# The S4D convolution and gated GLU kernel: one inverse stage in the first half's product, a second queue for some spectrum stores, and stage 1 in two PSUM pools

## The chip, the cores and the metric

The kernel runs on one core of a Trainium2 chip. The metric is the device time of one execution in microseconds (us), the median of three runs. Before the change it is 693.52 us (692.16 to 694.05). One further execution was taken with the profiler; its own time is 693.17 us.

## The reference, cut to what matters

The output is a gated mix of two branches over 2048 positions (L) and 448 channels (D). With u of shape 2048 x 448:

```python
g = sigmoid((u * gate_w).sum(-1, keepdims=True))
# branch a: S4D, a convolution as long as the sequence, N = 256 states per channel
K  = 2 * einsum("dn,dnl->dl", C, exp(A * dt * l)).real          # 448 x 2048
ya = irfft(rfft(u.T, 4096) * rfft(K, 4096))[:, :2048].T + u * D_skip
# branch b: GLU, F = 1792
yb = (sigmoid(x @ w_gate) * (x @ w_up)) @ w_down
out = g * ya + (1 - g) * yb
```

All data are float32.

## The kernel before, in words

**The work.** The channels are taken in two halves, h=0 and h=1, of 224 channels. For each half the kernel generates the filter K in 14 chunks (28 in all): TensorE multiplies small tables (tile `tp`), ScalarE turns them (lines L1228 to L1246), VectorE forms products (L1253, L1267, L1270), and TensorE contracts over the states into the tile `kp` (L1282). ScalarE evicts that to `ke` (L1303), and when a half's 14 chunks are there, four DMAs store it to the DRAM tensor `kd` (one tensor for each half, `kd0` and `kd1`; each store has 2048 rows of 56 floats). These 28 chunks fill the time from about 125 to 511 us. I call what follows the last `kp` the tail.

**The convolution** is a Fourier transform in two stages, a product of spectra, and the transform back. The class `Chain` does it for one half:
- `stage1` loads `kd` into `x` (named `fx_fu` for h=0 and `fx_fk` for h=1; 8 DMAs) and the tables `ft`, and runs eight blocks `stage1_four` (TensorE L813, ScalarE eviction L816).
- `transpose` turns 32x32 pieces of `x`: for h=0 through DRAM (four stores to `shf`, four loads, L832 to L836), for h=1 on VectorE (L827).
- `product` runs eight blocks `product_four` (L877 to L894). A block makes the second stage (TensorE L846, two PSUM tiles, z=0 and 1), multiplies the spectrum of u, `ua`, by it (VectorE L880), applies the first inverse stage (TensorE L890) and evicts (ScalarE L763). The spectrum of u lies in `ua` twice: in `ua[:, 0]`, and with real and imaginary rows exchanged in `ua[:, 1]`. A complex product is therefore two real products, and L890 adds them up in PSUM by two matrices that stand side by side in `m_sb`: eight matmuls a block, each of which the trace shows as two records (x16).
- `transpose` once more, then `back` (TensorE L927, VectorE L931) adds the result to the output.

PSUM tiles of the h=0 chain are in the pool `fups`, those of the h=1 chain in `fkps`. The trace names tiles by pool: `fps_fups` is a PSUM tile of h=0, `fps_fkps` one of h=1; `uax_fk` is h=0's `ua` and `ua_fk` h=1's.

**The GLU** fills TensorE between these steps: `glu_up` (tile `gu`, L1400 to L1405, 128x512 matmuls) and `glu_down` (tile `dn`, L1419 to L1423). ScalarE takes the tanh (L1384) and the casts; the weights and x are split into a high and a low part (L1365, L1367; L1332 to L1339).

**What sets the order.** Every step is registered by `op(engine, cost, ...)`. The table `PLACE` gives each step its place in its engine's queue, by (engine, tag, priority); `Plan.order` walks the queues and emits instructions in that order, and each engine runs its own in order. All DMAs are issued by SP (`dma`, L711), one after the other.

**The start.** `ones_pro` is set by VectorE (L1026); 48 matmuls on it (L1031) keep TensorE busy until the first GLU weights and x are there. The product code of `product_four`, word for word:

```python
for z in range(2):
    op("DVE", c_dve(2 * D, False), lambda z=z: V.tensor_mul(
        ua[:, :, z], ua[:, :, z], p[z][:, :D].unsqueeze(1).to_broadcast([128, 2, D])),
       [p[z]], [(ua, (c, z)) for c in range(2)], prio)
```

Of the kernel before, what the change touches and what calls it, by code (L numbers as in the profile page):

```python
# [28 lines left out]
    ('Act', 'aci', 10): (11, 39,),  # L29
    ('Act', 'aci', 19): (61, 88,),  # L30
    ('Act', 'acr', 10): (15, 37, 46,),
    ('Act', 'acr', 19): (63, 84, 98,),
# [26 lines left out]
    ('Act', 'dots', 1): (28,),  # L59
    ('Act', 'dots', 2): (50,),  # L60
    ('Act', 'dots', 16): (80, 81,),
# [18 lines left out]
    ('Act', 'idn', 10): (17,),  # L80
    ('Act', 'junk', 10): (34, 59,),
    ('Act', 'junk', 19): (76, 78, 113,),
# [12 lines left out]
    ('Act', 'pos_sb', 10): (65, 74,),  # L95
# [250 lines left out]
MOVE = True  # L346
# [357 lines left out]
def gated_mix(ctx: ExitStack, tc, u, ut, aim, cre, cim, ldt, dskip, gw,  # L704
# [60 lines left out]
    class Chain:  # L765
# [10 lines left out]
        def psum(self, k=0):  # L776
            return self.ps[k].tile("fps", self.bufs["fps"], (128, 512))
# [783 lines left out]
```

## Time and profile before

| | us |
|---|---|
| median of three runs | 693.52 |
| the profiled execution's own time | 693.17 |
| its span, first to last instruction | 691.4 |
| around the span (693.17 - 691.4) | 1.8 |
| TensorE (PE) busy | 678.0 |
| VectorE (DVE) busy | 603.4 |
| ScalarE (ACT) busy | 513.7 |
| GpSimd (POOL) busy | 276.4 |

The mean clock that TensorE was granted is 0.994 of full speed. A busy time is the time in which an engine worked; one that is busy over nearly the whole span leaves little room for waits. The chain of waits is the list of work that ended last, followed back from the end. Names in the trace leave buffer numbers out.

### The profile page before, as it was taken

How to read it: one execution, taken by the hardware profiler on the slowest of the kernel's cores; microseconds unless marked ns; L12 is line 12 of the kernel's file. 1: busy time of each engine (PE TensorE's matmuls, PEld its weight loads, DVE VectorE, ACT ScalarE, POOL GpSimd, SP SyncE). 2: the span in 40 equal slices, each digit the busy share in tenths (PEclk: the TensorE clock that was granted, in tenths of full speed). 3: DMA queues.
4: the chain of work that ended last, by engine and by line, in shares of the span. 5: the costliest groups of instructions: out<-in, count | busy, mean ns of one | idle time of the engine just before them, and what ended most of it. 6: DMA issues, size and time to landing. Idle time of an engine off the chain costs nothing.

```text
span 691.4 us, 16303 instructions
## 1 busy us (share of the span) xinstructions
PE 678.0 (98%) x6588; PEld 485.0 (70%) x6588; DVE 603.4 (87%) x705; ACT 513.7 (74%) x934; POOL 276.4 (40%) x280
## 2 busy tenths in 40 slices
PE   8999999999999999999999999999999999999996
PEld 7766667877876687675556667778878766556874
DVE  5999999999999999999999788999973479667976
ACT  5587799899999999999999999999942351342110
POOL 0215458556467758584665745758000000000000
PEclk9999999999999999998999999999999999999999
DMA  9768442646886784859966885355947973879966
GB/s 261 190 161 220 111 125 52 169 118 246 193 172 153 183 201 127 241 169 221 170 167 182 215 230 124 103 210 156 190 104 184 247 254 139 281 251 247 183 171 172
DMA packets 98771, 126.11 MB, mean 182 GB/s; under 512 B 31240, under 2 KB 81096, under 8 KB 97672
## 3 DMA queue, kind: packets, MB, share of 16 engines
q1 hardware_dynamic: 98696, 125.07, 69.2%
q8 instruction: 52, 0.85, 0.5%
q14 instruction: 23, 0.19, 0.1%
HBM read 81.46 MB, written 43.58 MB: 181 GB/s over the span
## 4 chain that ended last, share of the span: by engine, by line
PE 83%; ACT 9%; DVE 3%; DMA 2%; issue 1%; SPq 0%; ACTq 0%; DVEq 0%
PE gu_gps L1400 11%; PE gu_gps L1401 10%; PE gu_gps L1402 10%; PE dn_gps L1419 8%; PE kp_egp L1282 6%; PE dn_gps L1421 4%; PE tp_egp L1224 4%; PE dn_gps L1422 4%; PE dn_gps L1423 4%; PE tp_egp L1233 4%; PE fps_fups L813 3%; PE gu_gps L1404 3%; PE gu_gps L1405 3%; PE fps_fups L846 2%; PE fps_fups L890 2%; PE fps_fkps L890 2%
## 5 line engine op out<-in xcount | busy, mean ns | idle before, releaser
L1400 PE MATMUL gu_gps<-xs_glu,wh_glu 128*128 128x512 f32 x336 | 146.9, 437 | 0.4 <-DVE hh_glu L1386 0.3
L1401 PE MATMUL gu_gps<-xs_glu,wh_glu 128*128 128x512 f32 x336 | 132.4, 394 | 0.0
L1402 PE MATMUL gu_gps<-xs_glu,wl_glu 128*128 128x512 f32 x336 | 132.3, 394 | 0.0
L1270 DVE TENSOR_TENSOR cs_eg<-cs_eg,es_eg 128x2048 f32<-128x2048 f32 x56 | 130.3, 2326 | 1.3
L1214 POOL TENSOR_TENSOR tb_eg<-tb_eg 128x96 f32<-128x96 f32 (+2 forms) x84 | 115.0, 1372 | 5.9
L1253 DVE TENSOR_TENSOR es_eg<-tb_eg 128x1024 f32<-128x1024 f32 x112 | 111.4, 1016 | 2.2
L1400 PEld LDWEIGHTS gu_gps<-xs_glu,wh_glu 128*128 128x128 f32 x336 | 63.5, 189 | 29.7 <-issue 12.6
L1384 ACT ACTIVATE sg_glu<-gu_gps 128x512 f32<-128x512 f32 x56 | 34.0, 607 | 63.5 <-PE gu_gps L1405 60.4
L1267 DVE TENSOR_TENSOR cs_eg<-cs_eg,es_eg 128x1024 f32<-128x1024 f32 x56 | 70.6, 1260 | 10.9 <-ACT cs_eg L1246 7.7
L1230 ACT ACTIVATE nn_eg<-cs_eg 128x512 fp32r<-128x512 f32 x112 | 72.6, 648 | 6.0 <-PE tp_egp L1233 4.6
L1401 PEld LDWEIGHTS gu_gps<-xs_glu,wh_glu 128*128 128x128 f32 x336 | 63.6, 189 | 15.9 <-issue 5.6
L1402 PEld LDWEIGHTS gu_gps<-xs_glu,wl_glu 128*128 128x128 f32 x336 | 63.4, 189 | 15.0 <-DVE wl_glu L1367 0.5
L1217 POOL TENSOR_TENSOR tb_eg<-tb_eg,bs_eg 128x32 f32<-128x32 f32 x84 | 70.4, 841 | 5.8
L1228 ACT ACTIVATE cs_eg<-tp_egp 128x512 f32<-128x512 f32 x112 | 68.6, 618 | 3.2 <-DVE og L958 2.0
L1236 ACT ACTIVATE cs_eg<-tp_egp 128x512 f32<-128x512 f32 x112 | 68.4, 616 | 1.7 <-PE tp_egp L1233 1.5
L1235 ACT ACTIVATE cs_eg<-tp_egp 128x512 f32<-128x512 f32 x112 | 68.2, 618 | 1.5 <-PE tp_egp L1233 1.1
L1438 DVE SCALAR_TENSOR_TENSOR ob_glu<-dn_gps,og,ob_glu 128x448 f32<-128x448 f32 x72 | 48.7, 677 | 23.3 <-PE dn_gps L1423 21.3
L1246 ACT ACTIVATE cs_eg<-cs_eg,half_pi 128x1024 f32<-128x1024 f32 x56 | 66.1, 1180 | 0.5
L1204 POOL MEMSET tb_eg<- 128x96 f32 x28 | 7.8, 286 | 131.6 <-DVE es_eg L1253 124.2
L1282 PEld LDWEIGHTS kp_egp<-cs_eg 128*32 128x32 f32 x3584 | 51.3, 110 | 11.0 <-issue 8.6
L1282 PE MATMUL kp_egp<-cs_eg 128*32 128x64 f32 x3584 | 55.8, 220 | 0.1
L1421 PE MATMUL dn_gps<-vh_glu,hh_glu 128*128 128x448 f32 x136 | 52.3, 384 | 0.8 <-DVE ob_glu L1438 0.8
(161 smaller groups left out, 1338.7 us busy)
## 6 DMA issues: line engine op xcount, KB each, us to landing
shf<-fx_fu SPq DMA_DIRECT2D x16, 896.0 KB
fx_fu<-shf SPq DMA_DIRECT2D x16, 896.0 KB
us<-fx_fu SPq DMA_DIRECT2D x16, 896.0 KB
xr_glu<-in_w_dram SPq DMA_DIRECT2D x52, 256.0 KB
uax_fk<-us SPq DMA_DIRECT2D x16, 448.0 KB
ua_fk<-us SPq DMA_DIRECT2D x16, 448.0 KB
xr_glu<-in_w_dram SPq DMA_DIRECT2D x17, 224.0 KB
gt_pre<-in_u_dram SPq DMA_DIRECT2D x8, 448.0 KB
```

The costliest lines, as they stand in the source:

```text
L1214: pool(96 * m, lambda n=n, m=m: G.tensor_mul(g3(n + 1, m), g3(1, m), g3(n, 1).to_broadcast([128, 32, 3, m])))
L1217: pool(32, lambda e=e: G.tensor_mul(t(e + 1), t(e), b(3)))
L1228: op("Act", c_act(512, True), lambda: S.activation(cs[:, 1, ds, 32:96], block(tp), AF.Copy, bias=MAGIC), [tp], [(cs, ("s", i))], prio)
L1230: op("Act", c_act(512), lambda: S.activation(block(nn), cs[:, 1, ds, 32:96], AF.Copy, scale=-1.0, bias=MAGIC), [(cs, ("s", i))], [nn], prio)
L1253: V.tensor_mul(o.rearrange("p d (i k) -> p d i k", k=ny), x.unsqueeze(3).to_broadcast([128, 16, nx, ny]), y.unsqueeze(2).to_broadcast([128 ...
L1267: op("DVE", c_dve(1024), lambda: V.tensor_mul(cs[:, :, :, 0:32], cs[:, ::-1, :, 63:31:-1], es[:, :, 0:32].unsqueeze(1).to_broadcast([128, ...
L1270: op("DVE", c_dve(2048), lambda: V.tensor_mul(cs[:, :, :, 32:96], cs[:, :, :, 32:96], es[:, :, 32:96].unsqueeze(1).to_broadcast([128, 2, 1 ...
L1282: T.matmul(kp[32 * j:32 * j + 32, q], cs[:, z, 4 * j + q, 64:96], cs[:, z, 4 * j + q, 0:64], start=cs is parts[0] and z == 0 and q == 0, s ...
L1400: T.matmul(p.real, wh[:, k, cs], x[:, k], start=(k == 0), stop=False)
L1401: T.matmul(p.real, wh[:, k, cs], x[:, 4 + k], start=False, stop=False)
L1402: T.matmul(p.real, wl[:, k, cs], x[:, k], start=False, stop=False)
L1421: T.matmul(p[:, :D], hh[:, ts], vh.real, start=(i == 0), stop=False)
```

## The change

1. **The product of h=0** (`SWAP = (0,)`). Instead of two accumulated matrices, the sum of the two real products is made ahead of the inverse stage. ScalarE copies the spectrum tile from PSUM to a new SBUF tile `sw`, in four activations of 32 partitions each, that exchange neighbouring groups of 32 partitions and set the sign (L918). VectorE multiplies `ua[:, 0]` by the spectrum (L921), `ua[:, 1]` by `sw` (L923), and adds (L925), each 128x448. TensorE then applies one matrix: four matmuls a block (L933) instead of eight. The product of h=1 stays as it was (its line is now L905).
2. **The stores of `kd1`** with j=1 and j=3 are issued from ScalarE's queue; j=0 and 2 stay on SP.
3. **Stage 1 of h=1**: its blocks with odd b take their PSUM tiles from `fups` instead of `fkps` (`ks[1].other`).
4. **The first GLU loads**: x and w pieces are interleaved (`glu_first`).
5. **`PLACE`** is written anew as a whole, so every queue's order differs somewhat.

Lines of the changed kernel that the text speaks of: L825 stage 1, L858 second stage, L770 eviction, L969 back, L1068 `ones_pro`, L1458 to L1463 `gu`, L1479 to L1481 `dn`.

```diff
-    ('SP', 'kd1', 20): (267, 266, 268, 265,),
+    ('Act', 'kd1', 20): (827, 823,),
+    ('SP', 'kd1', 20): (262, 263,),
...
-    def dma(dst, src, size, r, w, prio, rate=ROW, issue=400.0, **kw):
-
-        return op("SP", size / rate, lambda: nc.sync.dma_start(dst(), src()), r=r, w=w, prio=prio, size=size,
+    def dma(dst, src, size, r, w, prio, rate=ROW, issue=400.0, eng="SP", **kw):
+
+        queue = nc.scalar if eng == "Act" else nc.sync
+        return op(eng, size / rate, lambda: queue.dma_start(dst(), src()), r=r, w=w, prio=prio, size=size,
...
+        def psum_one(self, b):
+            if self.other is None or b % 2 == 0:
+                return self.psum()
+            return self.other.tile("fps", FPS, (128, 512))
...
-            x, ps = self.x, [self.psum(), self.psum()]
+            x, ps = self.x, [self.psum_one(b), self.psum_one(b)]
...
             x, prio, p = self.x, self.prio, self.spectrum_four(b)
+            if self.h in SWAP:
+                self.product_swapped(ua, b, p)
+                return
...
+        def product_swapped(self, ua, b, p):
+            prio = self.prio
+            for z in range(2):
+                sw = self.tile("sw", (128, D))
+
+                def turn(z=z, sw=sw):
+                    for a in range(4):
+                        S.activation(sw[32 * a:32 * a + 32], p[z][32 * (a ^ 1):32 * (a ^ 1) + 32, :D], AF.Copy,
+                                     scale=1.0 if a % 2 else -1.0)
+                op("Act", 4 * PIECE, turn, [p[z]], [sw], prio)
+                op("DVE", c_dve(D, False), lambda z=z: V.tensor_mul(ua[:, 0, z], ua[:, 0, z], p[z][:, :D]),
+                   [p[z]], [(ua, (0, z))], prio)
+                op("DVE", c_dve(D), lambda z=z, sw=sw: V.tensor_mul(sw.real, ua[:, 1, z], sw.real),
+                   [(ua, (1, z))], [sw], prio)
+                op("DVE", c_dve(D), lambda z=z, sw=sw: V.tensor_add(ua[:, 0, z], ua[:, 0, z], sw.real),
+                   [sw], [(ua, (0, z))], prio)
+            y = [self.psum(1), self.psum(1)]
+
+            def f():
+                for z in range(2):
+                    for i in range(2):
+                        rows, to = slice(64 * i, 64 * i + 64), slice(64 * (i ^ z), 64 * (i ^ z) + 64)
+                        T.matmul(y[z][to, :D], m_sb[rows, 64:128], ua[rows, 0, z], start=True, stop=True)
+            op("PE", c_mm64(D), f, [(ua, (0, 0)), (ua, (0, 1)), m_sb], y, prio)
...
                 dma(lambda j=j: kd[hh].v("(a b) (j e) -> j a b e", b=64, j=4)[j], lambda j=j: ke[32 * j:32 * j + 32],
-                    32 * 64 * 224, [ke], [(kd[hh], j)], prio, SHORT, 3000.0)
+                    32 * 64 * 224, [ke], [(kd[hh], j)], prio, SHORT, 3000.0,
+                    "Act" if hh == 1 and j % 2 else "SP")
...
+    def glu_first(prio):
+        x = xs[0, 0] = glu.tile("xs", 2, (128, 7, 512), F32R)
+        parts = glu_w_parts(0, 0, prio)
+        for k in (0, 2):
+            glu_xk(x, k, 0, slice(0, 256), 0, prio)
+            next(parts)
+            glu_xk(x, k, 1, slice(256, 512), 256, prio)
...
-    glu_x(0, 0, 0)
-    glu_w(0, 0, 0)
+    glu_first(0)
...
+    ks[1].other = fups
     for h in halves:
         ks[h].stage1([kd[h]], lambda h=h: kd[h].v("(a b) d -> a b d", b=32))
         ks[h].transpose()
-        if h == 0 and MOVE:
-            ks[h].move(fk, (fups, fups), SX)
+    ks[0].move(fk, (fups, fups), SX)
+    for h in halves:
         ks[h].product(us[h])
```

**What the new order moves, at three places.** In the rows below a name ends in its buffer's number, `x2` counts equal instructions in a row, and no time is in them. First TensorE, at the inverse stage of the seventh and the second stage (L846, now L858) of the eighth of h=0's product blocks. Before (the four L890 rows of each half stand as two here, each of which comes twice):

```order
L890 MATMUL fps_fups_7318<-uax_fk_7190,m_sb 64x448 x2
L890 MATMUL fps_fups_7319<-uax_fk_7190,m_sb 64x448 x2
...
L890 MATMUL fps_fkps_7334<-ua_fk_7228,m_sb 64x448 x2
L890 MATMUL fps_fkps_7335<-ua_fk_7228,m_sb 64x448 x2
...
L846 MATMUL fps_fups_7347<-fx_fu_5148,m_sb 64x448 x2
L846 MATMUL fps_fups_7348<-fx_fu_5148,m_sb 64x448 x2
L846 MATMUL fps_fkps_7358<-fx_fk_6583,m_sb 64x448 x2
L846 MATMUL fps_fkps_7359<-fx_fk_6583,m_sb 64x448 x2
```

And of the change:

```order
L905 MATMUL fps_fkps_7387<-ua_fk_7270,m_sb 64x448 x2
L905 MATMUL fps_fkps_7388<-ua_fk_7270,m_sb 64x448 x2
...
L933 MATMUL fps_fups_7405<-uax_fk_7234,m_sb 64x448 x2
L933 MATMUL fps_fups_7406<-uax_fk_7234,m_sb 64x448 x2
L858 MATMUL fps_fkps_7416<-fx_fk_6545,m_sb 64x448 x2
L858 MATMUL fps_fkps_7417<-fx_fk_6545,m_sb 64x448 x2
L858 MATMUL fps_fups_7427<-fx_fu_5149,m_sb 64x448 x2
L858 MATMUL fps_fups_7428<-fx_fu_5149,m_sb 64x448 x2
```

The inverse stage of h=0 has two rows for a block where it had four; h=1's is as it was. Between a block's second stage and its inverse stage lies the multiply, here that of the seventh block. Before, VectorE had for a block of each half only:

```order
L880 TENSOR_TENSOR uax_fk_7190<-uax_fk_7190,fps_fups_7285 128x2x448
L880 TENSOR_TENSOR uax_fk_7190<-uax_fk_7190,fps_fups_7286 128x2x448
L880 TENSOR_TENSOR ua_fk_7228<-ua_fk_7228,fps_fkps_7295 128x2x448
L880 TENSOR_TENSOR ua_fk_7228<-ua_fk_7228,fps_fkps_7294 128x2x448
L1392 TENSOR_TENSOR hl_glu_7332<-sg_glu_7025,hh_glu_7311 128x512
```

and now (`7333` and `7334` are the block's two spectrum tiles; in brackets what a row waits for: Activation is ScalarE, DMAHW a DMA):

```order
L921 TENSOR_TENSOR uax_fk_7234<-uax_fk_7234,fps_fups_7333 128x448 [waits DMAHW4_49,PE_49,Activation_49]
L895 TENSOR_TENSOR ua_fk_7270<-ua_fk_7270,fps_fkps_7344 128x2x448 [waits DMAHW6_49,DMAHW1_49,PE_49]
L921 TENSOR_TENSOR uax_fk_7234<-uax_fk_7234,fps_fups_7334 128x448
L923 TENSOR_TENSOR swx_fk_7349<-uax_fk_7234,swx_fk_7349 128x448 [waits DMAHW0_49]
L895 TENSOR_TENSOR ua_fk_7270<-ua_fk_7270,fps_fkps_7343 128x2x448
L925 TENSOR_TENSOR uax_fk_7234<-uax_fk_7234,swx_fk_7349 128x448 [waits DVE_49]
L923 TENSOR_TENSOR swx_fk_7368<-uax_fk_7234,swx_fk_7368 128x448 [waits Activation_49]
L925 TENSOR_TENSOR uax_fk_7234<-uax_fk_7234,swx_fk_7368 128x448 [waits DVE_49]
```

The first multiply of a spectrum tile waits for ScalarE: it does not read the tile while ScalarE's four copies of it run.

Second, SP around the stores of `kd1`, before:

```order
L713 DMA kd_61<-ke_eg_4122 2048x1x56 x4
L713 DMA xr_glu_6550<-in_w_dram 128x448
L713 DMA xr_glu_6554<-in_w_dram 128x512
L713 DMA xr_glu_6560<-in_w_dram 128x512
L713 DMA fx_fk_6583<-kd_61 64x4x224
L713 DMA ft_fk_6588<-in_s1t_dram 128x512
```

and now on SP:

```order
L720 DMA kd_61<-ke_eg_4120 2048x1x56 x2
L720 DMA xr_glu_6483<-in_w_dram 128x512
L720 DMA xr_glu_6489<-in_w_dram 128x512
L720 DMA fx_fk_6545<-kd_61 64x4x224
L720 DMA ft_fk_6551<-in_s1t_dram 128x512
L720 DMA ft_fk_6559<-in_s1t_dram 128x512
L720 DMA fx_fk_6545<-kd_61 64x4x224 x5
```

with the other two stores on ScalarE, where they now stand between the GLU's own steps:

```order
L1345 ACTIVATE ke_eg_4120<-kp_egp_6357 128x4x64
L720 DMA kd_61<-ke_eg_4120 2048x1x56
L1449 ACTIVATE hh_glu_6458<-sg_glu_6428 128x512
L1423 ACTIVATE vh_glu_6466<-xr_glu_6015 128x448
L1442 ACTIVATE sg_glu_6473<-gu_gps_6436 128x512
```

SP's stores are halved, and the eight loads of `kd1` follow one another instead of standing between loads of `ua` and of weights.

Third, VectorE's first rows, before:

```order
L1184 MEMSET phs 1x512
L1026 MEMSET ones_pro_97 112x128
L1336 TENSOR_TENSOR xs_glu_136<-xr_pre_92,xs_glu_136 128x2x256
L1338 TENSOR_TENSOR xs_glu_136<-xr_pre_99,xs_glu_136 128x256
L1339 TENSOR_TENSOR xs_glu_136<-xr_pre_99,xs_glu_136 64x256
L1478 MEMSET half_pi 128x1
```

and now:

```order
L1068 MEMSET ones_pro_91 112x128
L1425 TENSOR_TENSOR wl_glu_139<-xr_pre_123,wh_glu_137 128x512
L1389 TENSOR_TENSOR xs_glu_135<-xr_pre_96,xs_glu_135 128x2x256
L1389 TENSOR_TENSOR xs_glu_135<-xr_pre_125,xs_glu_135 128x2x256
L1391 TENSOR_TENSOR xs_glu_135<-xr_pre_127,xs_glu_135 128x256
L1392 TENSOR_TENSOR xs_glu_135<-xr_pre_127,xs_glu_135 64x256
```

The memset of `phs` no longer stands ahead of that of `ones_pro`, and the first weights' low part comes ahead of x's.

More of the change, by code (lines that the diff above doesn't have):

```diff
@@ L28 @@
 PLACE = {
[L29 to L32, printed above, removed]
[26 rows of a table removed]
-    ('Act', 'dots', 1): (28,),
-    ('Act', 'dots', 2): (50,),
-    ('Act', 'dots', 16): (80, 81,),
[18 rows of a table removed]
-    ('Act', 'idn', 10): (17,),
-    ('Act', 'junk', 10): (34, 59,),
-    ('Act', 'junk', 19): (76, 78, 113,),
[12 rows of a table removed]
-    ('Act', 'pos_sb', 10): (65, 74,),
[22 rows of a table removed]
-    ('DVE', 'aci', 10): (50,),
-    ('DVE', 'aci', 19): (105,),
+    ('Act', 'aci', 10): (14, 38,),
+    ('Act', 'aci', 19): (61, 85,),
+    ('Act', 'acr', 10): (15, 36, 45,),
+    ('Act', 'acr', 19): (63, 83, 100,),
[26 rows of a table added]
+    ('Act', 'dots', 1): (27,),
+    ('Act', 'dots', 2): (46,),
+    ('Act', 'dots', 16): (79, 84,),
[18 rows of a table added]
+    ('Act', 'idn', 10): (16,),
+    ('Act', 'junk', 10): (28, 58,),
+    ('Act', 'junk', 19): (75, 77, 115,),
[13 rows of a table added]
+    ('Act', 'pos_sb', 10): (60, 74,),
[6 rows of a table added]
+    ('Act', 'swx', 40): (855, 856, 861, 862, 871, 872, 880, 881, 887, 889, 895, 897, 904, 905, 913, 914,),
[16 rows of a table added]
+    ('DVE', 'aci', 10): (43,),
+    ('DVE', 'aci', 19): (115,),
     ('DVE', 'acr', 10): (82,),
-    ('DVE', 'acr', 19): (150,),
+    ('DVE', 'acr', 19): (153,),
     ('DVE', 'ai', 10): (73,),
[14 rows of a table removed]
-    ('DVE', 'dtp', 10): (40,),
-    ('DVE', 'dtv', 10): (26,),
[6 rows of a table removed]
[14 rows of a table added]
+    ('DVE', 'dtp', 10): (56,),
+    ('DVE', 'dtv', 10): (33,),
[6 rows of a table added]
     ('DVE', 'f', 10): (14, 15,),
[2 rows of a table removed]
[2 rows of a table added]
     ('DVE', 'gs', 2): (119,),
[4 rows of a table removed]
-    ('DVE', 'half_pi', 0): (4,),
[24 rows of a table removed]
-    ('DVE', 'ones', 10): (1,),
-    ('DVE', 'p', 10): (18, 20, 21, 22, 23, 24, 25,),
-    ('DVE', 'phs', 20): (0,),
[6 rows of a table removed]
-    ('DVE', 'skip', 20): (35,),
[6 rows of a table removed]
-    ('DVE', 'uax', 40): (540, 544, 551, 552, 567, 565, 576, 575, 582, 581, 588, 587, 594, 595, 600, 599, 629, 630,
[26 rows of a table removed]
[4 rows of a table added]
+    ('DVE', 'half_pi', 0): (26,),
[24 rows of a table added]
+    ('DVE', 'ones', 10): (0,),
+    ('DVE', 'p', 10): (16, 17, 23, 25, 27, 29, 31,),
+    ('DVE', 'phs', 20): (8,),
[6 rows of a table added]
+    ('DVE', 'skip', 20): (49,),
+    ('DVE', 'swx', 40): (548, 547, 560, 561, 577, 574, 587, 588, 598, 600, 608, 611, 618, 621, 632, 634,),
[6 rows of a table added]
+    ('DVE', 'uax', 40): (546, 550, 545, 549, 559, 562, 558, 563, 575, 578, 570, 579, 585, 589, 586, 590, 594, 599,
[27 rows of a table added]
         1032, 1035, 1038, 1039, 1042,),
     ('PE', 'fps', -1): (0,),
[43 rows of a table removed]
[43 rows of a table added]
     ('Pool', 'bsx1', 10): (5, 11,),
@@ L346 @@
 MOVE = True
-SX = {'ft': 1, 'ua': 2, 'fps': 2}
-SK = {'ft': 2, 'ua': 2, 'fps': 3}
+SX = {'ft': 1, 'ua': 2, 'fps': 2, 'sw': 2}
+SK = {'ft': 2, 'ua': 2, 'fps': 3, 'sw': 2}
+SWAP = (0,)
+PIECE = 540.0
 K0D, LASTG, TN, TBB = False, 1, 4, 2
@@ L475, in run @@
         if o["size"]:
-            self.free[e] = t + (o["issue"] if e == "SP" else self.CAST)
+            self.free[e] = t + o["issue"]
             self.wire = max(self.wire, self.free[e] + 1000.0) + o["cost"]
@@ L769, in __init__ @@
             self.pool, self.ps, self.bufs, self.h, self.prio, self.on_dve = pool, (ps, ps), bufs, h, prio, on_dve
-            self.suffix = ""
+            self.suffix, self.other = "", None
             self.x = pool.tile("fx", 1, (128, 32, HD))
@@ L894, in product_four @@
                 evac(lambda r=2 * b + z: self.pair(r), y[z], [(x, 2 * b + z)], prio)
+        def product_swapped(self, ua, b, p):
[20 more added lines that the diff above has]
+            op("PE", c_mm64(D), f, [(ua, (0, 0)), (ua, (0, 1)), m_sb], y, prio)
+            for z in range(2):
+                evac(lambda r=2 * b + z: self.pair(r), y[z], [(self.x, 2 * b + z)], prio)
         def back(self, q):
@@ L1317, in glu_x @@
             glu_xz(x, z, t0, prio)
+    def glu_first(prio):
[5 more added lines that the diff above has]
+            glu_xk(x, k, 1, slice(256, 512), 256, prio)
+        for _ in parts:
+            pass
     def glu_xz(x, z, t0, prio):
@@ L1344, in glu_w, with glu_w_parts @@
     def glu_w(H, f, prio):
+        for _ in glu_w_parts(H, f, prio):
+            pass
+    def glu_w_parts(H, f, prio):
         wh, wl = (glu.tile(t, WB, (128, 4, 256), F32R) for t in ("wh", "wl"))
@@ L1354, in glu_w @@
             glu_split(wr, lambda wr=wr: wr.real, wh, wl, lambda t, k=k: t[:, k:k + 2], k, 512, prio, 7 * H + f // 2)
+            yield
         ws[H, f] = (wh, wl, vh, vl)
```

517 rows, old and new, of the table PLACE are left out of this document.

## The prediction

> **What bounds the kernel now.** I read the page's busy times first, then its slices, then the busy times by stage, then the chain of waits.
>
> ```profile
> span 691.4 us, 16303 instructions
> PE 678.0 (98%) x6588; PEld 485.0 (70%) x6588; DVE 603.4 (87%) x705; ACT 513.7 (74%) x934; POOL 276.4 (40%) x280
> PE   8999999999999999999999999999999999999996
> PEclk9999999999999999998999999999999999999999
> PE 83%; ACT 9%; DVE 3%; DMA 2%; issue 1%; SPq 0%; ACTq 0%; DVEq 0%
> ```
>
> TensorE works 678.0 of 691.4 us, and the chain is 83% TensorE: only 13.4 us of waits are left, so a change gains mainly by giving TensorE less work, and loses by making it wait. One slice has a lowered clock. The stages differ, in columns PE, PEld, DVE, ACT, POOL, clock, DMA share, GB/s:
>
> ```profile
> 125.00:511.00 386.00, 381.69 (x4911) 276.65 (x4910) 367.06 (x338) 370.11 (x676) 229.23 (x227) 0.99 0.69 175
> 511.00:691.00 180.00, 174.34 (x1066) 118.65 (x1065) 124.58 (x162) 48.99 (x95) 0.00 (x0) 1.00 0.78 213
> 546.00:636.00 90.00, 89.73 (x617) 52.80 (x616) 63.69 (x67) 33.37 (x66) 0.00 (x0) 1.00 0.74 237
> ```
>
> While the filter is generated, three engines are full (ScalarE 370.11, VectorE 367.06 of 386). In the product stretch, 546 to 636, TensorE is busy for 89.73 of 90 us while ScalarE has 56.6 us free and VectorE 26.3.
>
> **The change part by part.** Working against the profiled execution: 693.17 us, 1.8 of it around the span, 0.35 below the median of 693.52.
>
> *Fewer inverse matmuls.* The chain gives a block's inverse stage and its second stage:
>
> ```profile
> 549.96 1.66 PE fps_fups L890 x16
> 589.47 1.50 PE fps_fups L890 x16
> 559.20 0.91 PE fps_fups L846 x8
> 593.55 0.75 PE fps_fups L846 x8
> ```
>
> Sixteen records take 1.50 us, and 1.66 where the work before was the GLU's: going over to small matmuls costs 0.16. Eight records take 0.75 or 0.91 likewise. Eight blocks lose 1.50 - 0.75 each: **-6.0**. TensorE is full there, so this is on the path.
>
> *More switches.* Leaving small matmuls costs too:
>
> ```profile
> 538.00 1.03 PE L813 MATMUL fps_fkps<-fx_fk,ft_fk 64*128 64x224 f32 x8
> 538.96 0.47 PE L1421 MATMUL dn_gps<-vh_glu,hh_glu 128*128 128x448 f32 x1
> 539.27 0.36 PE L1422 MATMUL dn_gps<-vh_glu,hl_glu 128*128 128x448 f32 x1
> 539.47 0.37 PE L1423 MATMUL dn_gps<-vl_glu,hh_glu 128*128 128x448 f32 x1
> ```
>
> The first wide matmul is followed after 0.31, the next after 0.20: 0.10 to leave, 0.26 for a round trip. The new order has 88 groups of small matmuls among GLU work where there were 85: **+0.8**.
>
> *The start.*
>
> ```profile
> 0.91 0.48 DVE L1184 MEMSET phs<- 1x512 f32 x1 [0.91 <-PEq L1551]
> 1.46 0.17 DVE L1026 MEMSET ones_pro<- 112x128 f32 x1
> 1.68 8.10 PE L1031 MATMUL fps_fups<-ones_pro 112*128 112x128 f32 x48 [1.68 <-DVE ones_pro L1026]
> 8.62 0.63 ACT L1365 ACTIVATE wh_glu<-xr_pre 128x512 fp32r<-128x512 f32 x1 [2.23 <-DMA xr_pre<-in_w_dram]
> ```
>
> The memset of 0.48 leaves from ahead of the 48 matmuls. The 48 matmuls can start 0.48 earlier, and what follows them with them, if its data are there: the first GLU matmul needs a weight cast that ended at 9.25 us, because its load was late; that load now comes second instead of behind x's. **-0.5**; bounds 0 (loads no earlier) and -0.5.
>
> *The product's hidden work.* ScalarE's four copies of 32x448, twice a block, replace nothing; VectorE gets six 128x448 operations for two of 128x896.
>
> ```profile
> L880 DVE TENSOR_TENSOR uax_fk<-uax_fk,fps_fups 128x896 f32<-128x896 f32 x16 | 16.8, 1083 | 6.3 <-PE fps_fups L846 6.0 <-DMA uax_fk<-us 0.2
> L991 DVE TENSOR_TENSOR th_pro<-th_pro,ex_pro 128x448 f32<-128x448 f32 x4 | 2.5, 618 | 0.0
> L763 ACT ACTIVATE fx_fk<-fps_fkps 128x448 f32<-128x448 f32 x16 | 8.1, 543 | 14.7 <-PE fps_fkps L890 14.6
> 625.39 0.98 ACT L763 ACTIVATE fx_fu<-fps_fups 128x448 f32<-128x448 f32 x2 [4.49 <-PE fps_fups L890]
> ```
>
> A VectorE step takes 0.6 (0.618 in the row, half of 1.083 is 0.54). No row shows a 32-partition copy; the nearest, 448 columns on 128 partitions, takes 0.543 alone and 0.98 for two, 0.44 start to start. I take 0.44, bounds 0.44 and 0.54. Eight blocks give ScalarE 8 x 8 x 0.44 = 28 us and VectorE 8 x (6 x 0.6 - 2 x 1.08) = 11.5 us; 56.6 and 26.3 are free, so throughput suffices. What counts is each block's latency: from the end of the second stage to the inverse stage the new order leaves TensorE 8.9, 6.6, 8.5, 7.4, 6.1, 6.5, 6.3 and 6.0 us of other work (counts of the order times the rows' spacings, 0.23 for a `gu` matmul). VectorE's multiply and ScalarE's copies of one PSUM tile never overlap: one waits for the other. Block 7, whose rows stand above, is then a chain: four copies, multiply, h=1's multiply (1.08), multiply, four copies, multiply, add: 8 x 0.44 + 4 x 0.6 + 1.08 = 7.0, less 0.38 because the first tile is ready half a second stage earlier: 6.6 against 6.3. Block 5 has, beside the copies, five VectorE steps and an eviction by ScalarE (0.54) in its chain: 3.5 + 3.0 + 0.54 - 0.38 = 6.7 against 6.1. Block 2 has six steps: 6.7 against 6.6. In the other five ScalarE's second four copies run beside VectorE's first steps, 5 us or less against 6.0 and more, or TensorE has 7.4 and more. Waits of 0.4 + 0.5 + 0.2; a hand-over between engines takes some hundredths (the row's eviction starts 0.03 after the matmuls' end at 625.36): **+1.1**. With a copy at 0.54 each of the three waits 0.8 longer: +3.5.
>
> The Trainium skill ("PSUM — Partial Sum Buffer", section "PSUM bank collisions raise a hardware error") says that two engines must not access the same bank and group of 32 partitions together, reads included. By it the multiply could not be moved beside the copies; if the waits could go, the sum would be 1.1 lower. No row of before shows such a pair.
>
> *h=0's second transpose through DRAM.* After the last inverse stage of h=0:
>
> ```profile
> 625.36 1.50 PE fps_fkps L890 x16
> 626.39 0.32 SPq L713 DMA_DIRECT2D shf<-fx_fu  x1
> 630.79 7.18 SPq L713 DMA_DIRECT2D fx_fu<-shf  x4
> 652.00:654.00 2.00, 2.00 (x10) 1.50 (x10) 2.00 (x3) 0.00 (x0) 0.00 (x0) 1.00 1.02 345
> 654.00:656.00 2.00, 2.00 (x16) 1.39 (x16) 2.00 (x3) 0.00 (x0) 0.00 (x0) 1.00 0.03 11
> 655.20 0.91 PE fps_fups L927 x8
> 654.50 0.23 PE gu_gps L1400
> ```
>
> The eviction starts at 625.39 and the DMA engines fall from 345 to 11 GB/s at 654.0: 28.6 us, at most 29.8 by the use at 655.20. Before, TensorE had 29.8 us of work for that; now it has three `gu` matmuls (0.23) and one L890 group (1.50) fewer, one L846 group and a switch fewer (1.0), and four rows of h=1's `back` more (0.75): 27.4. The wait is 1.2 to 2.4; the data are in nearer the first, with a little for the signal: **+1.6**. What the rows don't bound is the queue: SP's four loads took 7.18 to issue, since each waits for the stores. If SP comes to them sooner the wait is 0; if other loads stand ahead of them longer it may be 5.
>
> *The rest* I put at nothing. Stores of `kd1`:
>
> ```profile
> 511.32 8.83 SPq L713 DMA_DIRECT2D kd<-ke_eg  x4
> 310.00 0.63 SPq L713 DMA_DIRECT2D kd<-ke_eg  x1
> 525.05 0.62 SPq L713 DMA_DIRECT2D fx_fk<-kd  x1
> ```
>
> Four in a row hold SP 8.83 us, one alone 0.63. The first load of `kd1` goes out at 525.05, 14.8 us after the last `kp` (510.25). Stage 1 of h=1 (538.00 in the row above, with no idle time ahead of it) stood behind some 27 us of TensorE work after that `kp`, and now stands behind 21.6, so even with stores as slow as now there are 6.8 us for a load. Two queues and two PSUM pools therefore shorten nothing that is waited for, and their gain is 0 too. The two stores now hold ScalarE 0.6 to 2.7 us each (8.83 - 0.63 over three); behind them stand the tanh and `hh` of the GLU, which TensorE needs for `dn`. ScalarE works 48.99 of 180 us in the tail, so 0; 2.7 without that cover.
>
> Sum: -6.0 + 0.8 - 0.5 + 1.1 + 1.6 = -3.0. 693.17 - 3.0 = 690.2, as a median 690.5.
>
> **The rivals.** A measurement of this kernel can tell about 0.3%, 2.1 us, from no change.
>
> *The gain ends as a wait ahead of the tail, or as lost clock.* The new order moves 2 `gu` and 6 `dn` (1.7 us) behind the last `kp`. If ScalarE and VectorE, full to 95%, set when the last `kp` comes, then that and the 0.5 of the start return: 690.2 + 2.2 = 692.4. Of the same size is a clock loss:
>
> ```profile
> 310.00:315.00 5.00, 3.54 (x17) 2.05 (x17) 5.00 (x6) 5.00 (x11) 0.00 (x0) 0.91 0.77 185
> 315.00:320.00 5.00, 5.00 (x14) 3.41 (x12) 4.96 (x8) 4.94 (x10) 1.71 (x4) 0.50 0.93 236
> 320.00:325.00 5.00, 5.00 (x136) 3.15 (x135) 4.67 (x4) 3.71 (x7) 4.84 (x4) 0.91 0.93 253
> 325.00:330.00 5.00, 4.63 (x26) 2.83 (x17) 4.47 (x4) 4.87 (x10) 1.73 (x3) 1.00 1.09 207
> ```
>
> TensorE idled 1.46 us, and the clock was then at half for 0.9 + 5 + 0.9 us (a mean of 0.91 in 5 us is 0.9 us at half): 3.4 lost. The 0.37 idle of the last row brought nothing of the kind. The wait of 1.6 at the transpose could do the same: 693.6. For the first speaks how full the two engines are; against it, that the chain is TensorE's for the most part and that TensorE itself works 381.69 of those 386 us. Either way the time stays within 0.3%.
>
> The Trainium skill ("TensorE: Matmul & The Clock Gate", section "Part 1: The HAM clock gate (the "warmup" mystery)") halves the clock after an idle window of about 3.4 us. By it a wait of 1.6 costs nothing more and the sum stays; the row, with 1.46 idle, speaks against it.
>
> *Slower: the swapped chain.* If a copy takes 0.54 start to start, blocks 2, 5 and 7 wait 0.9 to 1.4 each, 3.5 in all, and one of these idles, like the row's 1.46, brings the half clock (3.4): 690.2 + 2.4 + 3.4 = 696.0, median 696.3. It decides from about 0.5 a copy. For it speaks that copy and multiply of a tile stand one behind the other in the order; against it the 0.98 for two evictions.
>
> *Much faster: the new order loses the stall at 310 to 325.* The idle 1.46, its 3.4 of clock and the 0.37 after it make 5.2: 685.0, median 685.3. For it speaks that every queue is ordered anew around it, as the idle time is one of few left; against it, that the same engines are as full there as before, so that a stall can as well come up elsewhere.
>
> **How the numbers follow.** Forecast 0.38 (690.5), no difference 0.24 (692.7 to 693.9), slower chain 0.22 (696.3), stall gone 0.16 (685.3). Faster 0.54, same 0.24, slower 0.22. The forecast's own range is 688.9 (no wait at the transpose) to 693.0 (copies halfway to 0.54, +1.2; no gain at the start, +0.5; the transpose at 2.4, +0.8). The whole range takes in the last two cases with a little beyond, as copies and waits are bounded by neighbouring rows only: 684.0 to 697.5.
>
> **What would show it.** Eight L933 groups of 0.75 instead of 1.50; TensorE's first matmul near 1.2; idle ahead of the first `back` group of h=0, some 1.6; idle ahead of L933 in blocks 2, 5, 7 below 0.7; copies 0.44 apart; no idle ahead of stage 1 of h=1. A last `kp` as late as 510 means the second case; half clock in the tail the third.

## The result, and the profile after

The changed kernel takes 698.77 us (median of 5 runs, 696.86 to 701.35) against 693.52 before (5 runs, 692.16 to 694.68): a ratio of 1.0074, 95% interval 1.0047 to 1.0101. It is slower by 0.74%; the forecast was 690.5, and the time lies 1.3 us above the stated range. The profiled execution took 697.14 us, 4.0 more than that of before.

The page, for the changed kernel:

```profile
span 695.3 us, 16292 instructions
PE 675.1 (97%) x6524; PEld 484.7 (70%) x6524; DVE 618.1 (89%) x737; ACT 545.9 (79%) x998; POOL 270.6 (39%) x280
PE 69%; DVE 10%; ACT 10%; DMA 7%; issue 3%; SPq 0%; DVEq 0%; ACTq 0%
```

TensorE does 2.9 us less, in 64 records fewer, and yet the span is 3.9 longer. In the chain its share falls from 83 to 69%, while VectorE's rises from 3 to 10 and that of DMAs from 2 to 7: waits have come in. The product stretch, in the columns of the table by stage (PE, PEld, DVE, ACT, POOL, clock, DMA share, GB/s):

```profile
546.00:636.00 90.00, 85.66 (x524) 50.90 (x526) 73.89 (x104) 61.44 (x117) 0.00 (x0) 1.00 0.70 236
```

TensorE was busy for 89.73 of these 90 us and is now for 85.66. Neither ScalarE (28.6 us free) nor VectorE (16.1) is full. TensorE's waits behind the last `kp` (each with its total, its count and the longest), from the list of waits of the changed kernel:

```profile
PE fps_fkps L905 <- issue: 3.1, 2, 2.0
PE fps_fups L933 <- DVE uax_fk L925: 1.0, 1, 1.0
PE dn_gps L1479 <- DVE ob_glu L1496: 0.8, 1, 0.8
PE fps_fups L969 <- DMA fx_fu<-shf: 0.7, 1, 0.7
PE fps_fups L858 <- DMA fx_fu<-shf: 0.2, 1, 0.2
```

The wait for `ob_glu` was there before; the rest, 5.0 us, is new, and most of it stands ahead of the *other* half's inverse stage (L905 is h=1). What h=1 waits for is seen in VectorE's own rows, with ScalarE's and TensorE's beside them (start, duration, idle time ahead and what ended it):

```profile
596.07 0.62 DVE L921 TENSOR_TENSOR uax_fk<-uax_fk,fps_fups 128x448 f32<-128x448 f32 x1 [4.27 <-ACT swx_fk L918]
596.61 2.08 DVE L895 TENSOR_TENSOR ua_fk<-ua_fk,fps_fkps 128x896 f32<-128x896 f32 x2
598.83 0.62 DVE L921 TENSOR_TENSOR uax_fk<-uax_fk,fps_fups 128x448 f32<-128x448 f32 x1
```

```profile
593.86 2.17 ACT L918 ACTIVATE swx_fk<-fps_fups 32x448 f32<-32x448 f32 x4 [0.22 <-PE fps_fups L858]
596.63 2.17 ACT L918 ACTIVATE swx_fk<-fps_fups 32x448 f32<-32x448 f32 x4
```

```profile
593.58 1.08 PE L858 MATMUL fps_fkps<-fx_fk,m_sb 64*64 64x448 f32 x8
596.43 0.37 PE L1481 MATMUL dn_gps<-vl_glu,hh_glu 128*128 128x448 f32 x1
598.79 1.74 PE L905 MATMUL fps_fkps<-ua_fk,m_sb 64*64 64x448 f32 x16 [1.99 <-issue]
```

VectorE stands still for 4.27 us until ScalarE's four copies of the tile end at 596.03. Some 2.1 of these lie ahead of the copies' start at 593.86, when the second stage was not done; the copies themselves make up the rest. Behind the waiting multiply stand h=1's two multiplies, which need no copy and whose tiles were made by 594.66 (the first PE row); they end at 598.69, and TensorE, idle for 1.99, begins h=1's inverse stage at 598.79. The same happens once more at 621.25 (1.15).

### The profile page after: what moved, and what is told of

It reads as the page before. It is cut to its first block, busy times and chain, and to the rows that moved or that the text cites. A ratio compares the mean times of both kernels' runs of the same rounds, so it can differ in the third digit from the quotient of the medians.

```text
span 695.3 us, 16292 instructions
## 1 busy us (share of the span) xinstructions
PE 675.1 (97%) x6524; PEld 484.7 (70%) x6524; DVE 618.1 (89%) x737; ACT 545.9 (79%) x998; POOL 270.6 (39%) x280
## 4 chain that ended last, share of the span: by engine, by line
PE 69%; DVE 10%; ACT 10%; DMA 7%; issue 3%; SPq 0%; DVEq 0%; ACTq 0%
PE gu_gps L1458 8%; PE kp_egp L1324 7%; PE gu_gps L1460 7%; PE gu_gps L1459 7%; DMA fx_fu<-shf 4%; PE dn_gps L1477 4%; PE dn_gps L1479 4%; PE tp_egp L1266 4%; PE tp_egp L1275 4%; PE dn_gps L1480 3%; PE dn_gps L1481 3%; PE fps_fups L825 3%; PE fps_fups L858 3%; PE gu_gps L1462 2%; PE gu_gps L1463 2%
## 5 line engine op out<-in xcount | busy, mean ns | idle before, releaser
L1458 PE MATMUL gu_gps<-xs_glu,wh_glu 128*128 128x512 f32 x336 | 149.1, 444 | 0.3 <-ACT sg_glu L1442 0.2
L1256 POOL TENSOR_TENSOR tb_eg<-tb_eg 128x96 f32<-128x96 f32 (+2 forms) x84 | 113.2, 1352 | 5.9
L1458 PEld LDWEIGHTS gu_gps<-xs_glu,wh_glu 128*128 128x128 f32 x336 | 63.3, 188 | 34.4 <-issue 17.2
L1309 DVE TENSOR_TENSOR cs_eg<-cs_eg,es_eg 128x1024 f32<-128x1024 f32 x56 | 72.1, 1288 | 6.8 <-ACT cs_eg L1288 5.7
L1259 POOL TENSOR_TENSOR tb_eg<-tb_eg,bs_eg 128x32 f32<-128x32 f32 x84 | 63.8, 762 | 5.8
L1496 DVE SCALAR_TENSOR_TENSOR ob_glu<-dn_gps,og,ob_glu 128x448 f32<-128x448 f32 x72 | 48.7, 676 | 16.1 <-PE dn_gps L1481 13.5
L1324 PEld LDWEIGHTS kp_egp<-cs_eg 128*32 128x32 f32 x3584 | 52.8, 112 | 10.7 <-issue 6.9
L1324 PE MATMUL kp_egp<-cs_eg 128*32 128x64 f32 x3584 | 57.3, 223 | 0.0
L1275 PE MATMUL tp_egp<-nn_eg,idn 128*128 128x512 f32 x112 | 50.9, 454 | 3.7 <-ACT nn_eg L1272 3.6
L1479 PE MATMUL dn_gps<-vh_glu,hh_glu 128*128 128x448 f32 x136 | 52.6, 387 | 0.9 <-DVE ob_glu L1496 0.8
```

Source lines behind the costliest of these rows:

```text
L1256: pool(96 * m, lambda n=n, m=m: G.tensor_mul(g3(n + 1, m), g3(1, m), g3(n, 1).to_broadcast([128, 32, 3, m])))
L1275: op("PE", c_mm(532), lambda: T.matmul(tp.real, idn.real, nn.real, start=False, stop=True, skip_group_check=True), [nn, idn], [tp], prio)
L1309: op("DVE", c_dve(1024), lambda: V.tensor_mul(cs[:, :, :, 0:32], cs[:, ::-1, :, 63:31:-1], es[:, :, 0:32].unsqueeze(1).to_broadcast([128, ...
L1324: T.matmul(kp[32 * j:32 * j + 32, q], cs[:, z, 4 * j + q, 64:96], cs[:, z, 4 * j + q, 0:64], start=cs is parts[0] and z == 0 and q == 0, s ...
L1458: T.matmul(p.real, wh[:, k, cs], x[:, k], start=(k == 0), stop=False)
L1479: T.matmul(p[:, :D], hh[:, ts], vh.real, start=(i == 0), stop=False)
```

## The experiments

Each was timed in 5 rounds beside the kernel before. Theories: **S**, the swapped product makes the waits, either (S1) because copies and multiplies of a PSUM tile exclude each other and an in-order queue passes the wait on, or (S2) because ScalarE's copies take too long; **O**, the new order and the moved stores cost the time by themselves; later **P** and **T**, which part of the order. The kernel before, timed in the same rounds, had medians between 692.40 and 694.16, so kernels are compared by their ratios.

| kernel | median us | ratio to before, 95% |
|---|---|---|
| changed | 698.77 | 1.0074, 1.0047 to 1.0101 |
| e1 changed, unswapped | 698.54 | 1.0065, 1.0046 to 1.0085 |
| e2 before, swapped | 736.19 | 1.0609, 1.0586 to 1.0631 |
| e3 one copy | 692.93 | 0.9991, 0.9976 to 1.0006 |
| e4 no PSUM multiply | 694.73 | 1.0012, 0.9993 to 1.0031 |
| e5 before's order, then the changed tail, unswapped | 697.50 | 1.0058, 1.0040 to 1.0076 |
| e6 changed order, then before's tail, unswapped | 696.31 | 1.0038, 1.0020 to 1.0057 |
| e8 VectorE's order mended | 693.47 | 1.0007, 0.9988 to 1.0025 |
| e9 before's order, then e8's tail | 693.06 | 1.0005, 0.9986 to 1.0024 |
| e10 e8 with one pool | 696.79 | 1.0064, 1.0039 to 1.0089 |
| e11 e8 with all stores on SP | 693.50 | 1.0004, 0.9987 to 1.0021 |

**e1, the product as it was.** The places of the copies and of the added VectorE steps left the table.

```diff
-SWAP = (0,)
+SWAP = ()
```

> The changed kernel with the product of h=0 as it was before (eight inverse matmuls a block, no copies), the rest of the new order kept. Theory S (the swapped product's chain makes the waits): the 6.0 us of matmuls come back and some 6 us of waits in the product stretch go, so 697 to 699 us, with no idle time ahead of h=1's inverse stage. Theory O (the new order and the moved stores are worse by themselves): 698.8 + 6.0 = 704 to 705 us, with the waits still there.

698.54 us, as S said. But e1 does the same matmuls as before and is 4.5 us slower than before (0.65%, 0.46 to 0.85). So there are two effects: the swap by itself gives nothing (1.0074 against 1.0065), and the new order costs some 4.5 us, which is O's part. The 0.6 us between the two kernels is within the intervals, so the 6.0 that the swap saves goes in waits. My sum in the expectation for O had not seen that both can hold.

**e2, the swap in before's order.**

```diff
+            if self.h in SWAP:
+                self.product_swapped(ua, b, p)
+                return
```

> The kernel before with the swapped product of h=0 alone: copies, three VectorE steps and one matrix put at the places of the old multiply; order, stores and pools as before. Theory S: 693.5 - 6.0 + 4 to 9 of waits in the product stretch, 692 to 697 us, with idle time ahead of the inverse stages. Theory O: 693.5 - 6.0 = 687 to 689 us.

736.19 us, far from both. Before's order has, in five of the eight blocks, only 2.7 to 3.3 us of TensorE's work between h=0's second stage and its inverse stage (in its chain, for the fourth block, from 586.24 to 589.47), which the longer chain doesn't fit into, and I had placed the copies by hand. TensorE waits 12.7 us for VectorE ahead of that inverse stage in e2's list. The run shows that the swap doesn't go into before's order at these places; it tells nothing on S against O.

**e3, one copy a tile.** The exchange and the sign are left out.

```diff
-                    for a in range(4):
-                        S.activation(sw[32 * a:32 * a + 32], p[z][32 * (a ^ 1):32 * (a ^ 1) + 32, :D], AF.Copy,
-                                     scale=1.0 if a % 2 else -1.0)
+                    S.activation(sw.real, p[z][:, :D], AF.Copy)
```

> The changed kernel with one copy of 128x448 in place of the four of 32x448: the exchange of the 32-partition groups and the sign are left out. ScalarE then does 0.54 us a tile instead of 2.17. Theory S, in both forms (S1 the serial reading of PSUM, S2 ScalarE's time): most of the waits in the product stretch go, 692 to 694 us. Theory O: 698 to 699 us.

692.93 us, 0.83% below the changed kernel by the ratios: the copies carry what the swap loses, as both forms of S said. The two groups show the price, the changed kernel's and e3's:

```profile
L918 ACT ACTIVATE swx_fk<-fps_fups 32x448 f32<-32x448 f32 x64 | 34.3, 536 | 8.9 <-DVE uax_fk L921 3.9 <-issue 3.0 <-ACT sg_glu L1442 0.7
```

```profile
L917 ACT ACTIVATE swx_fk<-fps_fups 128x448 f32<-128x448 f32 x16 | 8.5, 543 | 11.7 <-DVE uax_fk L919 7.8 <-PE fps_fups L858 3.7
```

A copy of 32 partitions takes as long (536 ns) as one of 128 (543), and four in a row take 2.17 us: 0.54 start to start, no overlap.

**e4, no multiply from PSUM.** The real part of the product is left out.

```diff
-lambda z=z: V.tensor_mul(ua[:, 0, z], ua[:, 0, z], p[z][:, :D]),
-                   [p[z]], [(ua, (0, z))], prio)
+lambda z=z: V.tensor_mul(ua[:, 0, z], ua[:, 0, z], ua[:, 1, z]),
+                   [(ua, (1, z))], [(ua, (0, z))], prio)
```

> The changed kernel with VectorE's first multiply reading an SBUF tile (the other half of u's spectrum) instead of the spectrum in PSUM; it has the same size and place, and leaves the real part of the product out. Nothing but ScalarE reads the spectrum then. Theory S1 (copy and multiply of a PSUM tile exclude each other, and what stands behind a waiting one waits too): the waits shrink by more than half, 693 to 696 us. Theory S2 (ScalarE is too slow with 4.3 us of copies a block, so evictions and copies are late anyway): 698 to 699 us. Theory O: 698 to 699 us.

694.73 us: S1. ScalarE does all its copies as in the changed kernel (x64, 34.3 us), VectorE as many steps of the same size, and 0.62% by the ratios, 4.3 us, go. The multiply then waits no more for the second stage either, and e4 does not tell that wait from the one for the copies; in e8, below, the multiply reads the spectrum tile as in the changed kernel. The product stretch of e4:

```profile
546.00:636.00 90.00, 89.71 (x548) 54.59 (x548) 78.33 (x108) 64.25 (x122) 0.00 (x0) 1.00 0.74 249
```

TensorE is busy for 89.71 us again, with ScalarE's 64.25 above the 61.44 of the changed kernel.

**e5 and e6, the order in two halves**, both unswapped: each engine's queue is cut where the last `kp` stands.

```diff
-    glu_first(0)
+    glu_x(0, 0, 0)
+    glu_w(0, 0, 0)
```

(e5, with before's places up to there; e6 has the changed places up to there, before's behind, and in the code one pool and all stores on SP.)

> No swapped product. The order of before up to the last kp, then the changed kernel's order for all that follows, with its stores on two queues and its two PSUM pools. The unswapped changed kernel (e1) was 4.4 us slower than before. If that comes from the order after the last kp (first spectrum block moved there, more groups of small matmuls, the waits at stage 1 and at the second transpose): 696 to 699 us. If it comes from the order ahead of it: 693 to 695 us.

> No swapped product. The changed kernel's order (its start too) up to the last kp, then before's order, with before's stores on one queue and before's PSUM pools. Tail theory: 692 to 695 us, as before. Theory that the order ahead of the last kp costs the 4.4 us: 697 to 699 us.

e5, 697.50: the order of the tail costs 0.58% (4.0 us) by itself. e6, 696.31, costs too (0.38%). The two do not add up to e1. It may be that what the new order takes out of the filter's stretch stands, in e6, at the head of a tail that was not made for it; that was not tried, and e6's profiled execution (693.38) is the fastest of its twelve and shows only one new wait, of 1.0. With before's tail the cost of the new order's first half therefore stays open; with the new tail e1 against e5, and e9 below, show none.

**e8, another order of VectorE's queue**, the same operations. In six of the eight blocks VectorE now multiplies the tile that ScalarE copies second while ScalarE copies the first (in the changed kernel in three), and multiplies of h=1 and GLU steps change places with it. Eleven entries of VectorE's part of the table differ, those of no other engine; one of them:

```diff
-    ('DVE', 'uax', 40): (546, 550, 545, 549, 559, 562, 558, 563, 575, 578, 570, 579, 585, 589, 586, 590, 594, 599,
+    ('DVE', 'uax', 40): (548, 550, 547, 549, 560, 562, 556, 563, 572, 579, 575, 577, 586, 588, 584, 590, 597, 599,
```

> The changed kernel with the same operations; only the order of VectorE's queue in the product stretch differs: of a block's two spectrum tiles VectorE multiplies first the one that ScalarE copies second, and multiplies of h=1 and GLU steps no longer stand behind a multiply that waits for copies. Theory S1 (copies and multiplies of a tile exclude each other, and the in-order VectorE passes the wait on to h=1 and to TensorE): 6 to 9 us below the changed kernel, 690 to 693 us, and little idle time ahead of the inverse stages. Theory S2 (ScalarE's copies are too long whatever the order): 697 to 699 us.

693.47 us, 0.67% (4.6 us) below the changed kernel by the ratios (1.0007 against 1.0074): S1 again, though less than the 6 to 9 us that I had expected of it, and 0.5 us above its range. VectorE's waits in the product stretch, the changed kernel's and e8's:

```profile
DVE uax_fk L921 <- ACT swx_fk L918: 11.8, 5, 4.3
DVE swx_fk L923 <- ACT swx_fk L918: 2.0, 2, 1.7
```

```profile
DVE uax_fk L920 <- ACT swx_fk L917: 1.6, 1, 1.6
DVE swx_fk L922 <- ACT swx_fk L917: 1.6, 4, 0.5
```

The copies take as long as ever; the multiply waited for them in five blocks, 11.8 us in all, and now waits in one. The fifth block, which stood at 596 in the changed kernel, shows how:

```profile
592.55 0.62 DVE L920 TENSOR_TENSOR uax_fk<-uax_fk,fps_fups 128x448 f32<-128x448 f32 x1 [2.58 <-PE fps_fups L857]
593.41 2.09 DVE L894 TENSOR_TENSOR ua_fk<-ua_fk,fps_fkps 128x896 f32<-128x896 f32 x2 [0.24 <-PE fps_fkps L857]
592.75 2.18 ACT L917 ACTIVATE swx_fk<-fps_fups 32x448 f32<-32x448 f32 x4 [0.40 <-PE fps_fups L857]
```

One spectrum tile is multiplied and h=1's multiplies run while ScalarE copies the other tile. No wait ahead of an inverse stage is left in e8's list. How much of the gain is due to the order of the two tiles, and how much to h=1's and the GLU's steps, was not told apart.

**e9, before's order up to the last `kp`, then e8's.**

```diff
-    glu_first(0)
+    glu_x(0, 0, 0)
+    glu_w(0, 0, 0)
```

> The order of before (its start too) up to the last kp, then that of e8 with its swapped product. Theory P (what the new order moved behind the last kp, 2 gu and 6 dn, lengthens the tail, while the filter's stretch ends no earlier for it, as ScalarE and VectorE set its end): 1 to 3 us below e8 taken beside the same runs of before, so 690 to 692.5 us. Theory T (the order of the tail alone costs the 4 us): as e8, 693 to 694 us.

693.06 us, 1.0005 against e8's 1.0007: T. With this tail, what is moved out of the filter's stretch makes no difference. Beside e5 (same order up to `kp`, same tail but for the swap and VectorE's order) e9 is 0.53% lower: some 3.7 us, by the two intervals 1.8 more or less, is what the swap gives once hardly anything waits for it.

**e10 and e11, the parts that I had put at nothing**, each undone in e8.

```diff
-    ks[1].other = fups
```

> e8 (the swapped product with VectorE's order mended) with h=1's stage 1 in one PSUM pool, as before the change; order and stores as in e8. The prediction put the second pool at 0: then as e8, 693 to 694 us. If the new order needs it (its stage-1 blocks stand in pairs, so that with one pool the second of a pair waits for evictions): 695 to 700 us, with idle time between the blocks of stage 1.

```diff
-                    "Act" if hh == 1 and j % 2 else "SP")
+                    "SP")
```

> e8 with all four stores of kd1 issued by SP, as before the change; order otherwise as in e8. The prediction put ScalarE's queue at 0: then as e8, 693 to 694 us. If the new order needs it (its stage 1 comes 21.6 us after the last kp): 695 to 698 us, with a wait for the loads of kd1 ahead of stage 1.

e11 is e8 (1.0004): the second queue does nothing for the time. e10 is 0.57% slower than e8. Its rows show why, each second block of a pair:

```profile
531.14 1.40 PE L824 MATMUL fps_fkps<-fx_fk,ft_fk 64*128 64x224 f32 x10
532.84 1.02 PE L824 MATMUL fps_fkps<-fx_fk,ft_fk 64*128 64x224 f32 x6 [0.30 <-ACT fx_fk L827]
```

TensorE waits there for evictions (1.4 us in four waits in its list, and the first matmuls of a second block start late beside it). A pair takes 2.7 us from its first matmul to its end (531.14 to 533.86), where e8's first pair takes 1.8 (530.74 to 532.52); over four pairs this is the loss. Before, the blocks stood apart (538.00, 542.36, 548.85 and 551.56) and one pool was enough: the second pool is a need of the new order, no gain over the old one.

No kernel here beats before: e3 comes nearest and leaves work out, and e8, e9 and e11 cannot be told from it.

## Why the prediction was wrong

**The step that failed is "The product's hidden work", +1.1.** Its price and its reach were both off. With its 6.0 of saved matmuls it made the swap worth 4.9 us; measured, the changed kernel lies 0.6 above e1, so 5.5 of the 8.3 us between forecast and result are missing here, and most of the rest in the order (next step).
- *The price.* "I take 0.44, bounds 0.44 and 0.54": it was 0.54, the upper bound. The row with two evictions in 0.98 told nothing on four copies into one tile; the nearest row was the single one.
- *The reach.* I had found the serial chain and priced it as a wait of h=0's own inverse stage in three blocks (1.1, at most 3.5). That wait was 1.0 in all (567.15, ahead of L933). The larger one, 3.1, is that of h=1: its multiplies stand behind the waiting multiply in VectorE's queue. I had named what waits, and not who is queued behind it. The blocks were the right ones: the second waits 0.98 itself, and in the fifth and the seventh the wait falls ahead of h=1's stage, 1.99 and 1.15. These 4.1 in all stand against the 3.5 of the upper bound, so of the waits the price has the larger part and the reach the smaller. ScalarE, held by copies, also evicts later, and the second stage waits for PSUM: one group takes 1.58, with an eviction behind the copies ahead of its second half, where e1, e5 and e8 have 0.98:

```profile
587.49 1.58 PE L858 MATMUL fps_fkps<-fx_fk,m_sb 64*64 64x448 f32 x8
```

The waits and this group make 3.6 of the 5.5 (3.0 beyond the forecast 1.1, and 0.6); the rest stays open, and the intervals of the timing are about as wide. Shown: without the copies' length (e3) or without the multiply's reading of PSUM (e4) 5.8 and 4.3 us go, and by VectorE's order alone (e8) 4.6.

**The second step that failed is "More switches" as all that the order costs.** +0.8 was put for it; e1 says 4.5 in all, e5 4.0 in the tail. How these divide is read from traces, not tested. From the last `kp` to the span's end e5 takes 186.6 us (509.9 to 696.5), before 181.1 (510.3 to 691.4): 5.5 more in the two profiled executions, where the timing has 4.0. In it: h=0's first second stage, which ran ahead of the last `kp` before, and the round trips of four more groups, 0.75 + 4 x 0.26 = 1.8; the back stage's waits for transposed data and a table, 1.9; 0.2 more of small waits (0.5, and 0.3 before); and 0.4 by which one second-stage group, right behind h=1's, is longer than the usual 0.98. This last is there in the changed kernel (1.41 at 580.89), and in e1, e5 and e8, so the copies don't cause it. From e5:

```profile
PE fps_fups L966 <- DMA fx_fu<-shf: 1.4, 1, 1.4
PE fps_fups L966 <- DMA ftx_fk<-in_t1t_dram: 0.5, 1, 0.5
581.87 1.40 PE L855 MATMUL fps_fups<-fx_fu,m_sb 64*64 64x448 f32 x8
```

The remaining 1.2 stays open. The row of before that I had overlooked stands just ahead of the last `kp`:

```profile
507.41 0.98 PE L846 MATMUL fps_fups<-fx_fu,m_sb 64*64 64x448 f32 x8
508.32 1.99 PE L1282 MATMUL kp_egp<-cs_eg 128*32 128x64 f32 x128
```

I had counted groups over the whole program, where this one does not change; it changes sides.

The other terms:
- *Fewer inverse matmuls, -6.0*: right as work. The group has 64 records where it had 128, and e9 against e5, profiled, is 6.1 shorter from the last `kp` on (180.5 against 186.6). As a gain in time, 3.7.
- *The start, -0.5*: TensorE began 0.63 earlier and the GLU's first matmul came only 0.03 earlier (9.54 before, 9.51 after), though its data were there. But one pair of executions doesn't settle this term, as the last section shows, and no run times it alone.
- *h=0's second transpose, +1.6*: the wait came, 0.7.

```profile
661.50 0.98 PE L969 MATMUL fps_fups<-fx_fu,ftx_fk 128*64 128x224 f32 x8 [0.71 <-DMA fx_fu<-shf]
```

- *The stores at 0*: right. ScalarE's queue held 0.64 and 0.57 us, the first load went out 15.0 us after the last `kp` (14.8 before), stage 1 waited for nothing, and e11 agrees. *The two pools at 0* holds only against before's order (e10).
- *The rival of a gain lost ahead of the tail*: the last `kp` ended at 508.6 in the changed kernel's profile instead of 510.3. That alone shows little, as with the same order up to there it ended at 506.8 in e6's profile and at 510.1 in e4's; but e9 agrees with e8, so no loss is seen there with this tail.
- *The rival of the slower chain, 696.3*: its mechanism is what happened, from the price that it named, 0.5 a copy. Of its size, the half clock did not come; the waits of h=1 and the order did. The Trainium skill's rule on PSUM collisions ("PSUM — Partial Sum Buffer", section "PSUM bank collisions raise a hardware error"), which I had weighed as a bound, asks for such accesses to be kept apart: the program does so with ScalarE's and VectorE's reading of one tile, and e4, where VectorE leaves the tile alone, is 4.3 us faster here.
- *The rival of the lost stall*: the stall stayed, now at 325 to 335.

## What to carry to other kernels

When an engine that runs in order gets a step that can wait, price the wait for everything queued behind it, in the other half's chain too, before the wait of the step itself. Where, as here, the program keeps two engines' reads of a PSUM tile apart, and there are two such tiles, let each engine begin with another one: the second engine takes first the tile that the first will take last. And when an order is written anew, count what crosses the point from which the last stage alone sets the end, not the totals.

## What the runs showed of the hardware

**The clock did not fall after 1.99 us of idle time in the tail**, though it did after 1.46 in the trace of before. The changed kernel, at the largest wait and at the stall in the filter's stretch:

```profile
595.00:600.00 5.00, 3.02 (x25) 1.86 (x23) 3.77 (x5) 3.71 (x7) 0.00 (x0) 1.00 0.47 173
330.00:335.00 5.00, 2.90 (x11) 1.74 (x10) 4.92 (x7) 4.41 (x8) 4.09 (x7) 1.00 1.06 208
335.00:340.00 5.00, 5.00 (x136) 4.16 (x134) 5.00 (x6) 3.27 (x7) 4.69 (x5) 0.66 1.14 195
```

In the first row TensorE idled 1.98 of 5 us, in one piece, and the clock stayed whole there and after. In the second it idled 2.10, in pieces of up to 1.38, and the clock then stood at half for part of the next 5 us (a mean of 0.66). e1 has the same stall, with the same idle pieces (0.72 and 1.38 in these 5 us), and there the clock stayed whole:

```profile
330.00:335.00 5.00, 2.90 (x42) 1.65 (x44) 4.92 (x6) 4.42 (x9) 4.16 (x6) 1.00 0.96 184
335.00:340.00 5.00, 4.65 (x120) 3.21 (x110) 5.00 (x6) 4.02 (x8) 3.88 (x5) 1.00 1.14 210
```

So neither the length of one idle piece, from which I had worked the half clock out, nor the idle time in 5 us decides alone; what does, stays open. The Trainium skill's idle window of about 3.4 us ("TensorE: Matmul & The Clock Gate", section "Part 1: The HAM clock gate (the "warmup" mystery)") agrees with the tail and with e1, where no idle piece was that long and the clock stayed; read as a window that is idle throughout, it does not agree with the changed kernel's stall, where no piece was that long either and the clock fell.

**The moment of the full matmul rate differs from execution to execution, whatever the start.** Matmuls of `ones_pro` per microsecond, before and changed, are the count in the first pair of brackets:

```profile
6.00:7.00 1.00, 1.00 (x7) 1.00 (x7) 0.58 (x1) 0.39 (x1) 0.00 (x0) 1.00 0.86 269
7.00:8.00 1.00, 1.00 (x11) 1.00 (x11) 0.11 (x1) 0.00 (x0) 0.00 (x0) 1.00 1.07 335
```

```profile
6.00:7.00 1.00, 1.00 (x7) 1.00 (x7) 0.72 (x2) 0.81 (x2) 0.00 (x0) 1.00 0.95 344
7.00:8.00 1.00, 1.00 (x8) 1.00 (x8) 0.98 (x3) 0.89 (x2) 0.00 (x0) 1.00 1.04 379
8.00:9.00 1.00, 1.00 (x11) 1.00 (x10) 0.97 (x3) 0.96 (x3) 0.00 (x0) 1.00 1.05 340
```

Before, the rate goes from 6 or 7 in a microsecond to 11 at about 7 us from the span's start; in the changed kernel it is 8 between 7 and 8 us, and 11 only after that. The same 48 matmuls thus took 8.70 us where they had taken 8.10, and the 0.63 us by which TensorE began earlier was spent on more of them at the slow rate. But in e1, which begins as early as the changed kernel (1.05), the rate is 12 from 5 us on:

```profile
4.00:5.00 1.00, 1.00 (x9) 1.00 (x9) 0.00 (x0) 0.34 (x2) 0.00 (x0) 1.00 0.82 273
5.00:6.00 1.00, 1.00 (x12) 1.00 (x11) 0.54 (x1) 0.83 (x2) 0.00 (x0) 1.00 0.94 335
```

There the 48 took 7.22 us, and the GLU's first matmul came at 8.02. Over all profiled executions it came between 8.02 and 9.52 with the new start, and between 9.52 and 10.18 with before's. The clock column shows 1.00 throughout. What sets the moment was not tried.
